# Attention followed by an expert layer on one core: weights kept as float16 pairs, one pass over the token tiles, gates 1024 wide

## The chip, the core and the metric

The program runs on one core of a Trainium2 chip. Four engines matter here. TensorE (PE) multiplies matrices into PSUM, which has eight banks of 128 x 512 float32, and its weight loads are listed apart as PEld. VectorE (DVE) and GpSimd (POOL) do arithmetic element by element, ScalarE (ACT) does functions and casts, and SyncE (SP) only issues transfers. Each engine runs its own list of instructions strictly in order, and waits on semaphores for the others.

The metric is device time in microseconds (us) of one execution. The kernel before took 1372.12 us in the median of three runs (1371.07 to 1381.09). A second listing is of one execution under the hardware profiler, whose span is 1373.2 us.

## The reference

Inputs are q, k and v of 8 batches x 8 heads x 576 positions x 64, and two expert weights in float64. What is computed, cut to the core:

```python
scores = np.matmul(q, k.transpose(0, 1, 3, 2)) / np.sqrt(64)
scores = np.where(block_i >= block_j, scores, -1e9)   # blocks of 64 positions
attn = np.exp(scores - np.max(scores, axis=-1, keepdims=True))
attn = attn / (np.sum(attn, axis=-1, keepdims=True) + 1e-09)
x = np.matmul(attn, v)            # heads side by side: 4608 tokens x 512
h = x @ w_in                      # 512 x 2048
g = h * erf(np.maximum(h, 0.0) + np.log1p(np.exp(-np.abs(h))))
out = g @ w_out                   # 2048 x 512
```

In the text, "up" is h = x @ w_in, "gate" is the step from h to g, and "down" is g @ w_out. The 2048 columns of h are 16 chunks of 128.

## The kernel before

**Precision.** Each product of the expert layer is done as three matmuls on a high and a low part: up is whi with xh, whi with xl and wlo with xh (L349), down is whi and wlo with gh, and whi with gl (L370). Parts are in fp32r, a 32-bit form of rounded float32 that TensorE reads. The high part of the gate is a cast on ACT (L336), the low part a subtraction on POOL (L337).

**Weights.** They arrive as float64, read as pairs of 32-bit integers. `load_weight` turns a block of 128 x 512 into the two parts: VectorE works on the bits in five instructions (L294, L296, L299, L302, L304), ACT squares the upper words (L298) and casts the high part (L306), POOL subtracts and adds for the low part (L307, L308). There are 32 blocks, two for each chunk.

**Gate.** The function is approximated by a tanh (L320), four squares with scale and bias on ACT (L327), one product on VectorE (L331) and a last step on VectorE that adds a constant and multiplies by h (L335). Each works on 128 x 512 elements.

**Attention.** For each head, k and q are loaded (L464 to L467), their low parts subtracted on POOL (L470, L471), and scores multiplied a first time (L482) only for the row maxima, which VectorE reduces from PSUM (L486, L512). A small transpose (L516) and a cast and a transfer on ACT's queue (L518, L519) put the negated maxima into the operand of the second product (L535, L536). ACT takes the exponential (L542) and casts to float16 (L550); the low part is subtracted on VectorE for one half of the head and on POOL for the other (L552). Probabilities times v (L582) and the row sums (L608) are done for two heads at once; ACT copies the result out (L587). For every four heads a normalisation inverts the sums, spreads them by transposes (L644), multiplies (L647), splits x (L649, L650) and stores it to memory as `x_d` (L651).

**Two passes.** Memory on chip does not hold all weights in this form. A first pass takes chunks 0 to 5 (F1 = 6) over all 18 tiles of 256 tokens, in units of two chunks (54 units, one PSUM bank each for h). It runs between the heads, tile by tile as x becomes ready, and stores a partial sum to `part_d` (L686, L687). When attention is over, its buffers are closed and the remaining weights are decoded; this stretch is called the handover. A second pass (L817 to L840) takes chunks 6 to 15 over nine tiles of 512 tokens, one chunk a unit, reads `x_d` again (L391), fetches the partial sum (L834), adds it (L839) and stores the result (L840).

**Order.** The class `Plan` writes one order for all engines: each piece of work is a task with an engine, an assumed duration, a priority and the buffers that it takes. A simulated clock goes forward, and on each free engine the ready task with the lowest priority number for which buffers are free starts next. Heads have their number as priority; units of the first pass fill what is left.

## Time and profile before

| what | before |
|---|---|
| median of three runs | 1372.12 us (1371.07 to 1381.09) |
| profiled execution, span | 1373.2 us |
| mean granted TensorE clock | 0.930 |
| moved by transfers | 179.95 MB, mean 131 GB/s |
| read from and written to main memory | 112.29 MB and 37.75 MB |
| chain that ended last, by engine | PE 39%, DVE 4%, ACT 4%, issue 1%, DMA 1% |

The busy times by engine stand in the prediction. Three rows of the span in 40 equal slices of 34.3 us each show how the load shifts. Each digit is a busy share in tenths, for PEclk the clock that TensorE was granted:

```profile
PE   7776786998998988999999979889999999999997
DVE  4899889878887887888465326983323323233232
PEclk8766687999999999899999999999999999999998
```

Heads fill slices 1 to 19 or so, the rest of the first pass slices 20 to 24, the handover is around slice 25, and the second pass has the remainder. A share of busy time is how long an engine had an instruction under way; for TensorE, whose matmuls overlap, a digit of 9 does not say that it ran at its rate.

### The profile page before, as it was taken

What the parts mean: (1) busy time and instruction counts of PE and PEld (TensorE: products, weight loads), DVE (VectorE), ACT (ScalarE), POOL (GpSimd) and SP (SyncE); (2) the same over time, 40 slices, a digit from 0 to 9 for tenths busy, and PEclk for the clock granted to TensorE, in tenths of its full rate; (3) what the DMA queues carried; (4) which work ended last, traced back from release to release, by engine and by line L of the source; (5) the groups of instructions that cost most, each with busy time, mean ns of one, the idle gap of its engine ahead of it and who ended that gap; (6) DMA issues with size and microseconds to landing.
All of it is one profiled execution on the core that took longest, in us unless ns stands there. A gap on an engine that the chain in (4) does not pass through costs nothing. (4 is left out here: it accounts for less than half of the span.)

```text
span 1373.2 us, 21951 instructions
## 1 busy us (share of the span) xinstructions
PE 1253.6 (91%) x8168; PEld 1031.3 (75%) x8168; DVE 839.3 (61%) x1268; ACT 930.3 (68%) x1685; POOL 710.2 (52%) x521
## 2 busy tenths in 40 slices
PE   7776786998998988999999979889999999999997
...
DVE  4899889878887887888465326983323323233232
...
PEclk8766687999999999899999999999999999999998
...
GB/s 234 134 153 120 197 185 121 217 196 161 207 193 159 192 202 174 171 194 152 97 150 137 187 122 115 112 45 82 123 0 123 85 39 123 62 62 123 1 62 31
DMA packets 89371, 179.95 MB, mean 131 GB/s; under 512 B 8541, under 2 KB 27293, under 8 KB 89265
## 3 DMA queue, kind: packets, MB, share of 16 engines
...
q8 instruction: 65, 1.06, 0.3%
q10 hardware_dynamic: 640, 0.17, 0.1%
...
HBM read 112.29 MB, written 37.75 MB: 109 GB/s over the span
## 5 line engine op out<-in xcount | busy, mean ns | idle before, releaser
L327 ACT ACTIVATE m_r<-m_r,c 128x512 f32<-128x512 f32 x576 | 408.8, 721 | 84.9 <-DVE m_r L331 69.7
L337 POOL TENSOR_TENSOR m_gl<-m_r,m_gh 128x512 fp32r<-128x512 f32 x144 | 193.5, 1344 | 468.8 <-ACT m_gh L336 370.6
L331 DVE SCALAR_TENSOR_TENSOR m_r<-m_r,m_r 128x512 f32<-128x512 f32 x144 | 125.8, 874 | 293.9 <-ACT m_r L327 253.9
L349 PE MATMUL m_h<-xh,whi 128*128 128x256 f32 (+1 forms) x648 | 211.7, 327 | 1.3 <-DVE mx L486 1.0
L349 PE MATMUL m_h<-xl,whi 128*128 128x256 f32 (+1 forms) x648 | 208.7, 322 | 0.0
L349 PE MATMUL m_h<-xh,wlo 128*128 128x256 f32 (+1 forms) x648 | 208.6, 322 | 0.0
L370 PE MATMUL o<-whi,m_gh 128*128 128x512 f32 x432 | 176.0, 407 | 20.7 <-ACT m_gh L336 20.7
L486 DVE TENSOR_REDUCE mx<-s 64x1 f32<-64x288 f32 (+4 forms) x384 | 162.0, 465 | 49.3 <-PE s L482 49.0
L370 PE MATMUL o<-wlo,m_gh 128*128 128x512 f32 x432 | 172.6, 400 | 0.0
L335 DVE SCALAR_TENSOR_TENSOR m_r<-m_r,m_h 128x512 f32<-128x512 f32 x144 | 98.6, 685 | 116.9 <-ACT m_r L327 116.9
L542 ACT ACTIVATE p<-t 128x288 f32<-128x288 f32 (+4 forms) x384 | 130.2, 386 | 43.6 <-PE t L536 37.0
L320 ACT ACTIVATE m_r<-m_h,c 128x512 f32<-128x512 f32 x144 | 98.7, 686 | 80.5 <-PE m_h L349 79.9
L535 PE MATMUL t<-qk 69*128 69x288 f32 (+4 forms) x384 | 132.0, 353 | 17.0 <-DMA qk<-mt 10.7
L349 PEld LDWEIGHTS m_h<-xh,whi 128*128 128x128 f32 x648 | 126.0, 194 | 13.9 <-PE t L536 1.2
L349 PEld LDWEIGHTS m_h<-xl,whi 128*128 128x128 f32 x648 | 126.0, 194 | 10.8
L349 PEld LDWEIGHTS m_h<-xh,wlo 128*128 128x128 f32 x648 | 125.4, 194 | 8.7
L370 PE MATMUL o<-whi,m_gl 128*128 128x512 f32 x432 | 128.8, 400 | 1.4 <-POOL m_gl L337 1.3
L552 POOL TENSOR_TENSOR pl<-p,ph 128x768 f16<-128x768 f32 x64 | 114.6, 1790 | 28.0 <-ACT ph L550 26.3
L482 PE MATMUL s<-qk 68*128 68x256 f32 (+3 forms) x384 | 105.3, 365 | 22.7 <-DVE mx L486 7.8
L471 POOL TENSOR_TENSOR qk<-st,qk 64x576 fp32r<-64x576 f32 x64 | 109.9, 1719 | 28.7 <-DMA qk<-qk 18.4
L536 PE MATMUL t<-qk 128*128 128x288 f32 (+4 forms) x384 | 124.4, 334 | 0.0
L470 POOL TENSOR_TENSOR qk<-st,qk 64x576 fp32r<-64x576 f32 x64 | 105.5, 1652 | 21.5 <-DMA qk<-qk 15.2
...
## 6 DMA issues: line engine op xcount, KB each, us to landing
st<-qk SPq DMA_DIRECT2D x64, 288.0 KB
qk<-qk POOLq DMA_DIRECT2D x64, 288.0 KB, 4.7
qk<-qk SPq DMA_DIRECT2D x64, 288.0 KB
...
```

What stands on the lines that cost most here:

```text
L327: add("ACT", 722, lambda r=r, a=a, pp=pp: nc.scalar.activation(r[0](), a[0](), AF.Square, bias=const(pp[1]), scale=pp[0]), r=[a[1]], w=[r[1]])
L331: add("DVE", 890, lambda r=r, a=a, c=c, pp=pp, ops=ops: nc.vector.scalar_tensor_tensor(out=r[0](), in0=a[0](), scalar=pp[0], in1=c[0](), o ...
L337: add("POOL", 1450, lambda: nc.gpsimd.tensor_tensor(out=bgl(), in0=g[0](), in1=f32(bgh()), op=ALU.subtract), r=[g[1], bgh], w=[bgl])
L349: nc.tensor.matmul(hk()[:, k, :], lhsT=a(0)[:, cc * P : (cc + 1) * P], rhs=x()[:, cc, :], start=cc == 0 and i == 0, stop=cc == NCC - 1 and ...
L370: nc.tensor.matmul(o[c](), lhsT=a()[:, sl], rhs=b_(1), start=first and k == 0 and not lo and b_ is whi, stop=last and k == nu - 1 and lo)
L470: add("POOL", 1550, lambda: nc.gpsimd.tensor_tensor(out=t[:D, 0, :], in0=st()[:D, :], in1=f32(t[:D, 2, :]), op=ALU.subtract), r=[st] + Q(n ...
L471: add("POOL", 1780, lambda: nc.gpsimd.tensor_tensor(out=t[D:, 1, :], in0=st()[D:, :], in1=f32(t[D:, 1, :]), op=ALU.subtract), r=[st], w=Q( ...
L486: add("DVE", 145 + 1.07 * w_, lambda: nc.vector.tensor_reduce(out=mx[:r, col : col + 1], in_=s()[:r, c0 : c0 + w_], axis=AX.X, op=ALU.max, ...
L535: nc.tensor.matmul(s()[:kk, :w_], lhsT=kh[:K, ks], rhs=qh[:K, q0 : q0 + w_], start=True, stop=False)
L536: nc.tensor.matmul(s()[:kk, :w_], lhsT=klh[:, ks], rhs=qhl[:, q0 : q0 + w_], start=False, stop=True)
L542: add("ACT", 160 + 0.84 * (w_ - skip), lambda: nc.scalar.activation(p32s[pt][n % NP[pt]][:kk, c : c + w_ - skip], s()[:kk, skip:w_], AF.Ex ...
L552: add(eng, ns, lambda: on.tensor_tensor(out=pl(), in0=p, in1=ph(), op=ALU.subtract), r=keys + [ph], w=[pl])
```

## The change

All 16 chunks of both weights now stay on chip in one buffer `wsb`, as scaled float16 pairs, high and low part side by side. Decoding keeps the upper 32-bit word alone: ACT scales it (L309), VectorE takes exponent bits and sign in two 16-bit instructions (L311) and joins them by a shift and an or (L313). `measure_weights` finds the largest magnitude of each of the two weights (ACT L329), from which a power of two as a scale follows; then `split_weight` writes the high part on ACT (L320) and the low part on VectorE (L321). x is stored and read as a float16 pair too, scaled by the largest v of its batch, and the scales are undone in the tanh (L374) and at the store of the result (L753).

There is a single pass: 18 tiles of 256 tokens, each in four units of four chunks (72 units). A gate is 1024 wide, with h in two PSUM banks. Its last step writes back into PSUM (L394), and ACT and VectorE take the high and low part from there (L395, L396), so POOL has no part in it. The up matmuls are at L414, the down matmuls at L429, and the result goes straight to `out` (L754). The partial sums, the second reading of x and the handover are gone.

In attention there are three buffers for k and q instead of four, and three instead of four for the float16 probabilities. The copies of the product with v move to VectorE after the first batch (L640, L642). The normalisation multiplies into PSUM (L703), casts on ACT (L705) and subtracts on VectorE (L706). The planner's assumed durations change, and it now counts VectorE as slowed while POOL works (`SHARE`).

```diff
+                        if t.shares:
+                            ns += self.SHARE * max(0.0, free_at.get("POOL", 0.0) - now)
...
-    F1 = 6
...
-    T2 = 512
...
-    NB = 4
+    NB = 3
...
+    NK = 4
+    NU = NF // NK
+    UW = NK * T
...
-    NG, NR = 4, 2
-    HT = 14
+    NG, NR = 3, 2
...
-    x_d = tc.dram_tile((2, DM, NT), F32, name="x_d")
-    part_d = tc.dram_tile((NT, DM), F32, name="part_d")
+    x_d = tc.dram_tile((2, DM, NT), F16, name="x_d")
...
+    wsb = cpool.tile([P, (2 * NF + 1) * DM], F32, name="wsb")
...
+    def home(i):
+        return wsb[:, i * DM : (i + 1) * DM]
+
+    def place(s, f):
+        return f // NK * 2 * NK + s * NK + f % NK
+
+    def wf16(s, f, lo):
+        return home(place(s, f)).bitcast(F16)[:, lo * DM : (lo + 1) * DM]
+
+    def decode(s, f):
+
...
+        add("SP", 100, lambda: nc.sync.dma_start(words(), w[f, s].bitcast(I32)), w=[raw], lag=6000.0)
+        add("ACT", 670, lambda: nc.scalar.activation(val(), f32(top()), AF.Copy, scale=2.0**-112), r=[raw], w=[k])
+        for z, (op, val16) in enumerate(((ALU.logical_shift_right, 13), (ALU.bitwise_and, 0x8000))):
+            add("DVE", 420, lambda z=z, op=op, val16=val16: nc.vector.tensor_scalar(out=sign().bitcast(U16).rearrange("p (n t) -> p n t", t=2)[:, :, z],
+                in0=words().bitcast(U16).rearrange("p (n t) -> p n t", t=4)[:, :, 1 + 2 * z], scalar1=val16, scalar2=None, op0=op), r=[raw], w=[ks])
+        add("DVE", 700, lambda: nc.vector.scalar_tensor_tensor(out=bits(), in0=bits(), scalar=3, in1=sign(), op0=ALU.logical_shift_left, op1=ALU.bitwise_or), r=[ks], w=[k])
+
+    def split_weight(s, f):
+
+        i = place(s, f)
+        sc = wrow[:, 2 * s : 2 * s + 1]
+        kw, kv = ("W", i), ("W", i + 1)
+        add("ACT", 670, lambda: nc.scalar.activation(wf16(s, f, 0), home(i + 1), AF.Copy, scale=sc), r=[kv, ("wrow", s)], w=[kw])
+        add("DVE", 700, lambda: nc.vector.scalar_tensor_tensor(out=wf16(s, f, 1), in0=home(i + 1), scalar=sc, in1=wf16(s, f, 0), op0=ALU.mult, op1=ALU.subtract),
...
+        for i, h in enumerate(hs):
+            w = UW // len(hs)
+            for b, x, y in pieces(t):
+                add("ACT", 310 + 0.84 * w * (y - x) / T, lambda i=i, h=h, b=b, x=x, y=y, w=w: nc.scalar.activation(cut(br[0]()[:, i * w : (i + 1) * w], x, y), cut(h(), x, y), AF.Tanh,
+                    bias=const(p1), scale=bsc[:, 8 * b + 4 : 8 * b + 5]), r=ks[i] + [("bt", b)], w=[(br[0], i, b)])
...
-                add("ACT", 722, lambda r=r, a=a, pp=pp: nc.scalar.activation(r[0](), a[0](), AF.Square, bias=const(pp[1]), scale=pp[0]), r=[a[1]], w=[r[1]])
+                add("ACT", 300 + 0.834 * UW, lambda r=r, a=a, pp=pp: nc.scalar.activation(r(), a(), AF.Square, bias=const(pp[1]), scale=pp[0]), r=[a] + (first if k == 0 else []), w=[r])
...
-        g = regs[-1]
-        add("DVE", 680, lambda: nc.vector.scalar_tensor_tensor(out=g[0](), in0=g[0](), scalar=fin, in1=h(), op0=ALU.add, op1=ALU.mult), r=kh, w=[g[1]])
-        add("ACT", 620, lambda: nc.scalar.copy(bgh(), g[0]()), r=[g[1]], w=[bgh])
-        add("POOL", 1450, lambda: nc.gpsimd.tensor_tensor(out=bgl(), in0=g[0](), in1=f32(bgh()), op=ALU.subtract), r=[g[1], bgh], w=[bgl])
+        r, w = regs[-1], UW // len(hs)
+        for i, h in enumerate(hs):
+            cs = slice(i * w, (i + 1) * w)
+            kh = [k for k in ks[i] if isinstance(k, tuple)]
+            add("DVE", 690, lambda cs=cs, h=h: nc.vector.scalar_tensor_tensor(out=h(), in0=r()[:, cs], scalar=end, in1=h(), op0=ALU.add, op1=ALU.mult), r=[r] + ks[i], w=kh)
+            add("ACT", 620, lambda cs=cs, h=h: nc.scalar.copy(bgh()[:, cs], h()), r=ks[i], w=[(bgh, i)])
+            add("DVE", 690, lambda cs=cs, h=h: nc.vector.tensor_tensor(out=bgl()[:, cs], in0=h(), in1=bgh()[:, cs], op=ALU.subtract), r=ks[i] + [(bgh, i)], w=[(bgl, i)])
...
+        hs = [bank(f"{name}_h{i}") for i in range(nb)]
+        hold = token("h", NH)
...
+                def go(k=k, cc=cc, f=f):
+                    for i, (lo, x) in enumerate(((0, xh), (0, xl), (1, xh))):
+                        nc.tensor.matmul(hk(k), lhsT=wf16(0, f, lo)[:, cc * P : (cc + 1) * P], rhs=x()[:, cc, :], start=cc == 0 and i == 0, stop=cc == NCC - 1 and i == 2)
+                add("PE", 3 * mmns(T, True), go, r=[("W", place(0, f)), ("Wl", place(0, f)), xh, xl], w=[(hs[k * T // 512], k), hold])
...
+                    pairs = ((gl, 0),) if lo else ((gh, 0), (gh, 1))
+
+                    def go(c=c, lo=lo, f=f, sl=sl, pairs=pairs, k=k):
+                        for a, wlo in pairs:
+                            nc.tensor.matmul(o[c](), lhsT=a()[:, sl], rhs=wf16(1, f, wlo), start=u == 0 and k == 0 and not lo and wlo == 0, stop=u == NU - 1 and k == NK - 1 and lo)
+                    add("PE", len(pairs) * mmns(DM, True), go, r=[(gl if lo else gh, k * T // 512), ("W", place(1, f)), ("Wl", place(1, f))], w=[o[c], oh[c]], off=0.001 * (8 * lo + k))
...
+            x = buf("x", [P, NCC, T], F16, nm, f"{nm}_{t}")
...
-            add("ACT", 470, lambda: nc.scalar.activation(usb()[:, q0:q1], u()[:, : q1 - q0], AF.Copy, scale=vsb()[:, :1]), r=[u, vsb], w=[(usb, hf)])
+            if qd < NQ:
+                add("ACT", 470, lambda: nc.scalar.copy(usb()[:, q0:q1], u()[:, : q1 - q0]), r=[u], w=[(usb, hf)])
+            else:
+                add("DVE", 430, lambda: nc.vector.tensor_copy(usb()[:, q0:q1], u()[:, : q1 - q0]), r=[u], w=[(usb, hf)])
...
-                add("DVE", 550 - 200 * hf, lambda q0=q0, q1=q1, rb=rb: nc.vector.tensor_tensor(out=f32(xs()[:, 1, q0:q1]), in0=usbs[pp]()[:, q0:q1], in1=rb()[:, : q1 - q0], op=ALU.mult),
-                    r=[rb, (usbs[pp], 0), (usbs[pp], 1)], w=[(xs, hf)])
-            add("DVE", 450, lambda: nc.vector.tensor_copy(xs()[:, 0, :], f32(xs()[:, 1, :])), r=[(xs, 0), (xs, 1)], w=[(xs, 2)])
...
+                add("ACT", 500 - 160 * hf, lambda q0=q0, q1=q1, rb=rb, w=w: nc.scalar.copy(x16()[:, 0, q0:q1], rb()[:, :w]), r=[rb], w=[(x16, 0, hf)])
+                add("DVE", 550 - 200 * hf, lambda q0=q0, q1=q1, rb=rb, w=w: nc.vector.tensor_tensor(out=x16()[:, 1, q0:q1], in0=rb()[:, :w], in1=x16()[:, 0, q0:q1], op=ALU.subtract),
...
+        for u in range(NU):
+            moe_unit(t, u, at[u])
...
+            add("ACT", 700, lambda ob=ob, c=c, sc=sc: nc.scalar.activation(ob(), o[c](), AF.Copy, scale=sc), r=[o[c], oh[c], *ks], w=[ob])
+            add("SP", 100, lambda ob=ob, q=q: nc.sync.dma_start(out[q : q + P, :], ob()), r=[ob], lag=3000.0)
...
+    for s in range(2):
+        for f in range(NF):
+            plan.prio = DEC0[s] + f * DECR[s]
+            decode(s, f)
+        plan.prio += 0.5 * DECR[s]
+        measure_weights(s)
+    for u in range(NU):
+        for s in range(2):
+            for f in range(u * NK, (u + 1) * NK):
+                plan.prio = MOE + u * STEP + s * DOWN - SPLIT
+                split_weight(s, f)
+
...
-            moe_unit(w2, xs[i], o, tw, 1, u, f"m2_{t}_{u}", u == 0, u == nu, u != nu, oh, 3, "g", at, 0.0)
-            if u == nu:
-                for c, pt in enumerate(pts):
-                    add("DVE", 700, lambda c=c, pt=pt, o=o: nc.vector.tensor_tensor(out=pt(), in0=o[c](), in1=pt(), op=ALU.add), r=[o[c], oh[c]], w=[pt])
-                    add("SP", 100, lambda c=c, pt=pt, t=t: nc.sync.dma_start(out[t + c * P : t + (c + 1) * P, :], pt()), r=[pt], lag=3000.0)
...
+        for t in range(NTT):
+            if t not in x1 and ready(t) <= n + 1:
+                plan.prio = n
+                x1[t] = load_x(t)
+                token_tile(t, [max(ready(t), MOE + (t * NU + u) * STEP) for u in range(NU)])
```

Three places show how the order moves. The first is VectorE early in the program. Rows name the line, the operation and output<-inputs with the shape; `mx` are row maxima, `pl` the low part of probabilities, `raw`, `bits` and `sq` a weight block on its way. Before:

```order
L552 TENSOR_TENSOR pl0_0_431<-p32_0_0_111,ph0_0_414 128x832
L512 TENSOR_TENSOR mx1_124<-mx1_124 64x1
L294 TENSOR_SCALAR bits1_0_444<-raw1_0_146 128x512
L296 SCALAR_TENSOR_TENSOR bits1_0_444<-raw1_0_146,bits1_0_444 128x512
L299 SCALAR_TENSOR_TENSOR sq1_0_353<-sq1_0_353,bits1_0_444 128x512
L486 TENSOR_REDUCE mx0_123<-s01_4_459 128x1 x2
L486 TENSOR_REDUCE mx0_123<-s2_4_464 128x1
L552 TENSOR_TENSOR pl0_1_481<-p32_0_1_112,ph0_1_454 128x832
L486 TENSOR_REDUCE mx0_123<-s3_4_466 128x1
L486 TENSOR_REDUCE mx0_123<-s4_4_0_472 64x1
```

After, from about the same head on (`sign` and `wsb` are a weight block):

```order
L311 TENSOR_SCALAR sign0_2_447<-raw0_2_143 128x512 x2
L313 SCALAR_TENSOR_TENSOR wsb_94<-wsb_94,sign0_2_447 128x512
L538 TENSOR_REDUCE mx0_123<-s01_4_422 128x1 x2
L311 TENSOR_SCALAR sign0_3_481<-raw0_3_146 128x512 x2
L313 SCALAR_TENSOR_TENSOR wsb_94<-wsb_94,sign0_3_481 128x512
L538 TENSOR_REDUCE mx0_123<-s2_4_426 128x1
L604 TENSOR_TENSOR pl0_1_498<-p32_0_1_112,ph0_1_400 128x832
L538 TENSOR_REDUCE mx0_123<-s3_4_430 128x1
L538 TENSOR_REDUCE mx0_123<-s4_4_0_440 64x1
L311 TENSOR_SCALAR sign0_4_551<-raw0_4_330 128x512 x2
L313 SCALAR_TENSOR_TENSOR wsb_94<-wsb_94,sign0_4_551 128x512
```

Before, one block is begun and its chain stands among maxima and low parts; after, three blocks pass in eleven rows, each in two rows between the maxima of heads 3 and 4, and the low part of head 1 comes behind two of them.

The second is ACT in the middle of the heads, with a gate before (`m1_5_1` is tile 5, second unit of the first pass; `t` are products to be exponentiated, `p32` their results):

```order
L320 ACTIVATE m1_5_1_r0_6670<-m1_5_1_h_6553,c1_85 128x512
L327 ACTIVATE m1_5_1_r0_6670<-m1_5_1_r0_6670,c2_87 128x512
L327 ACTIVATE m1_5_1_r1_6694<-m1_5_1_r0_6670,c3_89 128x512
L327 ACTIVATE m1_5_1_r1_6694<-m1_5_1_r1_6694,c4_91 128x512
L550 CAST ph1_45_6715<-p32_1_1_114 128x768
L542 ACTIVATE p32_1_0_113<-t1_46_128_6641 128x448
L327 ACTIVATE m1_5_1_r1_6694<-m1_5_1_r1_6694,c5_93 128x512
L320 ACTIVATE m1_5_2_r0_6740<-m1_5_2_h_6673,c1_85 128x512
L327 ACTIVATE m1_5_2_r0_6740<-m1_5_2_r0_6740,c2_87 128x512
L327 ACTIVATE m1_5_2_r1_6757<-m1_5_2_r0_6740,c3_89 128x512
L336 CAST m1_5_1_gh_6762<-m1_5_1_r1_6694 128x512
```

And after, with the gates of tile 6 (a tile that spans two batches takes two tanh instructions for each bank):

```order
L602 CAST ph0_35_7078<-p32_0_1_112 128x832
L602 CAST ph1_35_7088<-p32_1_1_114 128x768
L374 ACTIVATE m6_0_r0_7133<-m6_0_h0_7062,c1_84,bsc_98 128x2x192
L374 ACTIVATE m6_0_r0_7133<-m6_0_h0_7062,c1_84,bsc_98 128x2x64
L374 ACTIVATE m6_0_r0_7133<-m6_0_h1_7099,c1_84,bsc_98 128x2x192
L374 ACTIVATE m6_0_r0_7133<-m6_0_h1_7099,c1_84,bsc_98 128x2x64
L383 ACTIVATE m6_0_r0_7133<-m6_0_r0_7133,c2_86 128x1024
L383 ACTIVATE m6_0_r1_7185<-m6_0_r0_7133,c3_88 128x1024
L383 ACTIVATE m6_0_r1_7185<-m6_0_r1_7185,c4_90 128x1024
L374 ACTIVATE m6_1_r0_7220<-m6_1_h0_7135,c1_84,bsc_98 128x2x192
L374 ACTIVATE m6_1_r0_7220<-m6_1_h0_7135,c1_84,bsc_98 128x2x64
L383 ACTIVATE m6_0_r1_7185<-m6_0_r1_7185,c5_92 128x1024
```

The gate of 512 columns is one tanh and four squares among exponentials and casts of heads; the gate of 1024 is four shorter tanhs and squares of twice the width, and a cast of head 35 stands ahead of it.

The third is TensorE between heads. Before (`rb` are the spread sums of a normalisation, `mt` the small transpose of a head's maxima, `o1_3_0` an output bank of tile 3):

```order
L644 MATMUL rb3_1_1_0_5060<-ident_74,rw3_1_1_4982 128x128 x3
L644 MATMUL rb3_1_1_1_5064<-ident_74,rw3_1_1_4982 128x128
L644 MATMUL rb3_1_1_1_5064<-ident_74,rw3_1_1_4982 128x64
L516 MATMUL mt35_5068<-ident_74,mx1_124 5x128
L370 MATMUL o1_3_0_4948<-whi3_1350,m1_3_1_gl_4980 128x512
L582 LDWEIGHTS vh4_0_4433
L582 MATMUL u8_0_1_5078<-ph0_32_4739,vh4_0_4433 64x320
```

After, between two units of tile 4 (`t` products to be exponentiated, `s` scores for maxima, `rt` the row sums turned for a normalisation, `m4_3_h0` a bank of h):

```order
L587 MATMUL t3_29_320_5787<-qk2_105 128x256
L588 MATMUL t3_29_320_5787<-qk2_105 128x256
L534 MATMUL s01_31_5790<-qk1_104 128x256 x2
L534 MATMUL s2_31_5793<-qk1_104 128x384
L534 MATMUL s3_31_5795<-qk1_104 128x512
L534 MATMUL s4_31_0_5803<-qk1_104 64x288
L587 MATMUL t4_29_320_5805<-qk2_105 64x256
L588 MATMUL t4_29_320_5805<-qk2_105 64x256
L681 MATMUL rt3_0_5810<-sel_109,rs0_117 128x4 x3
L681 MATMUL rt3_0_5810<-sel_109,rs1_118 128x4 x3
L414 LDWEIGHTS wsb_94
L414 MATMUL m4_3_h0_5822<-xh_4_5255,wsb_94 128x256
```

Before, one down matmul stands alone between the work of heads. After, scores and products of heads 31 and 29 and a normalisation follow one another, and then the up matmuls of tile 4's last unit begin, with weights from `wsb`.

More of the change, by code (lines that the diff above doesn't have):

```diff
@@ L13 @@
 I32 = mybir.dt.int32
-U32 = mybir.dt.uint32
+U16 = mybir.dt.uint16
 F32R = mybir.dt.float32r
@@ L351, in moe_unit @@
[L351 to L352 removed]
+        for k in range(NK):
+            f = u * NK + k
             for cc in range(NCC):
[L354 to L359 removed]
```

381 lines of the change are left out of this document (153 added, 228 removed).

## The prediction

> **What bounds the kernel now.** I read the page's engine shares first, then busy time by stage, then the chain that ended last, then TensorE's timeline for what one matmul costs when nothing holds it up. The page first:
>
> ```profile
> span 1373.2 us, 21951 instructions
> PE 1253.6 (91%) x8168; PEld 1031.3 (75%) x8168; DVE 839.3 (61%) x1268; ACT 930.3 (68%) x1685; POOL 710.2 (52%) x521
> ```
>
> TensorE's 91% is not 91% of its possible rate, as matmuls overlap in the records. Busy time by stage follows (the start to head 16, the heads with the first pass between them, the handover, the second pass), and for some stages the busy time of single lines: the transposes of L516, one for each head, and the two matmul lines of the MoE.
>
> ```profile
> core 0: us, PE busy (x) PEld busy (x) DVE busy (x) ACT busy (x) POOL busy (x), PEclk, DMA share, GB/s
> 0.00:196.00 196.00, 150.78 (x1042) 109.01 (x1043) 160.05 (x246) 92.01 (x199) 139.92 (x119) 0.73 0.66 169
> 250.00:650.00 400.00, 373.74 (x3376) 314.16 (x3375) 325.61 (x552) 289.76 (x613) 300.74 (x209) 0.95 0.71 186
> 850.00:915.00 65.00, 53.19 (x213) 40.76 (x212) 61.21 (x68) 48.96 (x81) 40.48 (x28) 0.95 0.24 77
> 950.00:1350.00 400.00, 400.00 (x1767) 331.20 (x1766) 125.34 (x175) 291.14 (x443) 94.42 (x73) 1.00 0.20 69
> ```
>
> L516 in the start and with the heads, then L349 and L370 with the heads:
>
> ```profile
> 0.00:196.00 196.00, 5.74 (x17) 1.62 (x17) 0.73 0.66 169
> 250.00:650.00 400.00, 11.26 (x42) 3.53 (x42) 0.95 0.71 186
> 250.00:650.00 400.00, 79.29 (x522) 72.52 (x522) 0.95 0.71 186
> 250.00:650.00 400.00, 76.08 (x246) 43.89 (x246) 0.95 0.71 186
> ```
>
> In the second pass TensorE never rests. In the handover and at the start VectorE is the full one (61.21 of 65, 160.05 of 196). With the heads no engine is full: VectorE 81%, POOL 75%, ACT 72%. What a matmul costs in a dense stretch stands in the chain (start, length, count) and in TensorE's timeline:
>
> ```profile
> 707.48 2.89 PE m_h L349 x24
> ...
> 972.73 2.72 PE o L370 x12
> ```
>
> ```profile
> 395.73 0.33 PE L582 MATMUL u<-ph,vh 128*64 128x320 f16 x2
> 395.89 0.30 PE L582 MATMUL u<-ph,vl 128*64 128x320 f16 x2
> ...
> 396.84 0.30 PE L582 MATMUL u<-pl,vh 128*64 128x320 f16 x2
> ...
> 397.53 0.41 PE L535 MATMUL t<-qk 69*128 69x320 f32 x1
> ...
> 403.03 0.30 PE L535 MATMUL t<-qk 69*128 69x288 f32 x1
> ...
> 404.89 0.40 PE L370 MATMUL o<-whi,m_gh 128*128 128x512 f32 x1
> ...
> 409.64 1.06 PE L482 MATMUL s<-qk 68*128 68x256 f32 x6
> 410.54 0.28 PE L349 MATMUL m_h<-xh,whi 128*128 128x256 f32 x1
> ...
> 411.36 0.30 PE L582 MATMUL u<-ph,vh 128*64 128x256 f16 x2
> ...
> 411.76 0.22 PE L582 MATMUL u<-ph,vl 128*64 128x128 f16 x2
> 411.82 0.22 PE L582 MATMUL u<-pl,vh 128*64 128x128 f16 x2
> ...
> 412.91 0.33 PE L582 MATMUL u<-ph,vh 128*64 128x320 f16 x2
> ```
>
> A 512-wide fp32r matmul costs 2.72 / 12 = 226.7 ns, a 256-wide one 2.89 / 24 = 120 ns: twice the columns cost 107 ns more, so 0.417 ns a column and 13 ns fixed. The float16 pairs of 320 columns start 0.95 / 7 = 136 ns apart from 395.89 to 396.84: 133.3 ns of columns and only 2.5 fixed. One head costs TensorE 0.90 us for the six score matmuls (409.64 to 410.54), 1.86 for the probabilities and a small transpose (403.03 to 404.89), and half of 1.80 (395.73 to 397.53) and 1.55 (411.36 to 412.91) for probability times v and the sums of a pair: 4.4, with 0.2 taken for the rare transposes of the normalisation 4.6 us.
>
> So from 250 to 650 TensorE did 522 L349 matmuls at 120 ns, 246 of L370 at 227 ns and 42 heads (x522, x246, x42): 63 + 56 + 193 = 312 us of work in 400. I call that a rate share of 0.78. In the second pass it is 1767 x 226.7 ns = 400 in 400: 1.00. The loss sits where TensorE waits in order for engines that are all half busy, at the start, and in the handover.
>
> **The change, by parts.** The profiled span lies 1.1 us over the median of the runs (1372.1), so I predict against it directly. It falls into a start of 196 us, the heads with the first pass to some 650, the rest of that pass to 850, the handover to 915 and the second pass. The new span is a start, heads 17 to 63 with units between them, and the units left over.
>
> *Matmuls of the MoE.* Before there are 1296 up matmuls of 256 and 1080 of 512 columns, and 1728 down matmuls: 156 + 245 + 392 = 793 us. After there are 3456 of 256 columns and 1728 of 512, all float16: 3456 x 109.2 ns + 1728 x 215.8 ns = 377 + 373 = 750 us. Gain 43 us where TensorE is full. The 256-wide tiles load twice the weights per column of the second pass; in the rows at 411.76 and 411.82 two loads and two 128-column matmuls take 0.06 us, so a load hides under 109 ns.
>
> *The start.* VectorE sets it. The price of the old decoding, by block and by shape:
>
> ```profile
> L296 DVE SCALAR_TENSOR_TENSOR bits<-raw,bits 128x512 int32<-128x512 int32 x32 | 42.5, 1328 | 0.9
> L299 DVE SCALAR_TENSOR_TENSOR sq<-sq,bits 128x512 f32<-128x512 f32 x32 | 40.0, 1250 | 2.1 <-ACT sq L298 0.8
> ...
> L294 DVE TENSOR_SCALAR bits<-raw 128x512 int32<-128x512 int32 x32 | 34.5, 1078 | 1.1 <-DMA raw<-w 1.1
> ...
> L304 DVE SCALAR_TENSOR_TENSOR bits<-raw,bits 128x512 f32<-128x512 uint32 x32 | 31.7, 990 | 0.9
> ...
> L302 DVE TENSOR_SCALAR bits<-sq 128x512 int32<-128x512 int32 x32 | 20.6, 645 | 0.9
> ```
>
> That is 5.29 us a block, and 8 of the 32 blocks lie in the first 196 us. The new chain is two halves of 512 in 16 bits (nearest L302, 0.645), one shift-and-or and later one subtraction (nearest L304, 0.99, without POOL less: I take 0.85). By the order after, all 32 decodings, some 12 subtractions, 17 heads and two gates stand on VectorE before head 17, where the units flow on TensorE. Before, 160 us in 196 held 8 blocks (42) and 17 heads, so 6.9 us a head; after: 17 x 6.9 + 32 x 2.14 + 12 x 0.85 + 8 = 204 us, and at the 82% that VectorE reached before (160.05 of 196) 249. POOL no longer splits weights there, so I take 245 instead of 196: 49 us lost. Ends: 204 if VectorE were full, 283 if each of the three operations of a block cost as L296 (32 x 0.85 more, at 82%).
>
> *Heads 17 to 63.* By the order after, TensorE now has 2496 up and 1224 down matmuls there: 273 + 264 + 46 x 4.6 = 748 us. Is another engine longer? The rows:
>
> ```profile
> L327 ACT ACTIVATE m_r<-m_r,c 128x512 f32<-128x512 f32 x576 | 408.8, 721 | 84.9 <-DVE m_r L331 69.7 <-ACT m_r L327 0.4
> ...
> L331 DVE SCALAR_TENSOR_TENSOR m_r<-m_r,m_r 128x512 f32<-128x512 f32 x144 | 125.8, 874 | 293.9 <-ACT m_r L327 253.9 <-POOL m_gl L337 39.9
> ...
> L320 ACT ACTIVATE m_r<-m_h,c 128x512 f32<-128x512 f32 x144 | 98.7, 686 | 80.5 <-PE m_h L349 79.9
> L335 DVE SCALAR_TENSOR_TENSOR m_r<-m_r,m_h 128x512 f32<-128x512 f32 x144 | 98.6, 685 | 116.9 <-ACT m_r L327 116.9
> ...
> L336 ACT CAST m_gh<-m_r 128x512 fp32r<-128x512 f32 x144 | 87.8, 610 | 23.0 <-DVE m_r L335 19.7 <-PE o L370 3.2
> ...
> L542 ACT ACTIVATE p<-t 128x448 f32<-128x448 f32 x64 | 34.4, 537 | 9.5 <-PE t L536 8.6
> ...
> L542 ACT ACTIVATE p<-t 128x192 f32<-128x192 f32 x64 | 21.0, 327 | 2.1 <-PE t L536 1.8
> ```
>
> An ACT element costs (537 - 327) / 256 = 0.82 ns, so a 1024-wide square 721 + 420 = 1.14 us, and the gate of a unit 2 x 0.686 + 4 x 1.14 + 2 x 0.61 = 7.2 us, where two old gates took 8.4. ACT's own work for a head is at most the page's 930 less the gates' 595, over 64: 5.2. Each head also queues a small DMA on ACT, and the next operation waits for it:
>
> ```profile
> 342.11 0.70 ACTq L519 DMA_DIRECT2D qk<-mt  x1
> 342.85 0.26 ACT L518 CAST mt<-mt 5x128 fp32r<-5x128 f32 x1 [0.77 <-ACT mt L518]
> ```
>
> So at most 51 x 7.2 + 46 x 5.9 + 18 for the stores = 657 us: 88% of TensorE's 748. VectorE takes the subtraction for the low half over from POOL (L337 goes): 51 x (1.2 + 4 x 0.685) + 46 x 6.9 = 518. The normalisation, once for a pair of heads, drops a cast and POOL's subtraction and adds two subtractions on VectorE and two casts on ACT; the two copies of u move from ACT to VectorE after the first batch. Four more VectorE operations a pair, each at most L335's 0.685, are 63 us over 46 heads: 581, 78%. ACT's two casts take the place of the two copies. POOL, 75% before, loses its work for the MoE. TensorE is the fullest, and its units stand ready from earlier tiles. The query and key buffers go from four to three, so a head's loads start two heads ahead instead of three:
>
> ```profile
> qk<-qk POOLq DMA_DIRECT2D x64, 288.0 KB, 4.7
> ```
>
> 4.7 us to land, a copy after it and POOL's subtractions fit into two heads of 17 us, so I cost it at nothing; if heads came every 6 us it would show. The share lies between 0.78 (before, with heads) and 1.00 (second pass). I take 0.94, nearer the second, since TensorE now queues and the others wait: 748 / 0.94 = 796 us.
>
> *The rest.* After the last head's transpose stand 816 up and 456 down matmuls: 89 + 98 + some 7 of attention = 194, at 0.99 196. A gate (from its second half 0.7 + 3.5 + 1.2 + 1.1 + 0.7 + 0.6, about 8 us) hides under the 10.4 us of one up and one down between a unit's own two; if ACT is late, TensorE waits there. No handover, no second pass, no partial sums through memory; DMA falls to one reading of x in float16, and is no bound (0.71 of its share with the heads before). The load of x for tile 15 waits on SP behind the last stores of x; ahead of it TensorE has three blocks of 5.2 us, against some 12 of normalisation and two transfers, so 0 to 10 us, taken as 0. The last gate uncovers some 4 us, and a store follows: 10.
>
> Sum: 245 + 796 + 196 + 10 = 1247 us.
>
> One rule weighs against this. The Trainium skill, "TensorE: Matmul & The Clock Gate", section "Back-to-back issue gap", says that a stream of weight load and matmul pairs holds some 81 ns a matmul at 128 columns where the streaming alone is 56, so that loads show. Taken as 25 ns on each of 5184 matmuls it would make the sum 1247 + 130 = 1377; the rows at 411.76 and 411.82 (0.06 us with two loads) disagree.
>
> **Rivals.** *Slower: the share stays at 0.78.* Two 1024-wide units hold four of eight PSUM banks, the outputs two or three more; a head's matmuls find one or two, so TensorE stands in order behind an exp or a max. For it: 0.78 with smaller units. Against: there VectorE and POOL were 81% and 75% full, and lose that. Price 748 / 0.78 = 959, time 1410 (959 + 451); it decides against the change below a share of 0.81 (1373) and is slower by over 1% below 0.80.
>
> *In between: share 0.81 to 0.87*, by ACT's long gate squares standing in order ahead of an exp that TensorE waits for: ACT is second at up to 88%. Against: it has a tenth to spare. 1310 to 1373.
>
> *Faster: share 0.98 and VectorE full at the start*: 204 + 763 + 194 + 6 = 1167. For it: the second pass's 1.00. Against: VectorE was never full at the start.
>
> *Weight loads show.* If float16 with a load per matmul keeps the 13 ns of fp32r, 5184 x 10.5 ns = 54 us more: 1301. For it: no row shows a 128-column float16 load under 256 columns; against, the pairs above.
>
> *The change does nothing of the sort*: ruled out, the order after has one up and one down per tile and chunk.
>
> **How the numbers follow.** Forecast (share 0.88 to 0.97, start 225 to 270): 0.57, own range 1200 to 1325. Fast rival 0.11. In between 0.14, of which 0.03 within 1%. Loads show 0.06. Share under 0.81: 0.12, of which 0.09 slower by over 1%. The range 1165 to 1350 leaves out about 0.04 below and 0.16 above. A difference of 1% is about what a measurement of this kernel can tell. Faster 0.85, same 0.06, slower 0.09.
>
> **What would show it.** Right: float16 pairs at 109 and 216 ns in the last 190 us; head 17's transpose at 225 to 270 us with VectorE over 75% before it; a head every 17 us after; no part_d or second reading of x. Wrong: spacings over 115 ns; waits of TensorE on ACT (exp) or VectorE (max) of over 100 us in the middle; ACT over 95% there; TensorE's clock under 0.95 after 250 us.

## The result, and the profile after

The changed kernel took 1312.91 us in the median of four runs (1309.82 to 1316.28), against 1371.59 us for the kernel before (1369.07 to 1381.09 in four): a ratio of 0.9553, 95% interval 0.9517 to 0.9589. It is 59 us faster where 125 us were forecast. 1312.9 us lies in the range given (1165 to 1350), but the gain is less than half of the one forecast. The profiled execution has a span of 1308.0 us.

The changed kernel's page, its engine shares, the granted clock in 40 slices of 32.7 us, and what the transfers moved:

```profile
PE 1192.5 (91%) x9254; PEld 835.8 (64%) x9254; DVE 778.4 (60%) x1433; ACT 895.5 (68%) x1485; POOL 348.8 (27%) x280
PEclk8667676889999999999999999999999999999999
DMA packets 69468, 123.38 MB, mean 94 GB/s; under 512 B 7073, under 2 KB 34017, under 8 KB 69360
HBM read 74.52 MB, written 18.87 MB: 71 GB/s over the span
```

TensorE is again at 91%, ACT as before at 68%, POOL at 27% for 52%. Transfers moved 123 MB for 180. The clock row shows the kernel's weak place: all of its low digits lie in the first nine slices.

Busy time by stage of the changed kernel (start to head 17's small transpose, head 17 to 18, heads 18 to 63, the rest):

```profile
core 0: us, PE busy (x) PEld busy (x) DVE busy (x) ACT busy (x) POOL busy (x), PEclk, DMA share, GB/s
0.00:260.60 260.60, 181.89 (x1207) 125.08 (x1207) 196.05 (x375) 145.97 (x293) 99.17 (x96) 0.72 0.62 166
260.60:314.00 53.40, 42.44 (x308) 26.78 (x306) 29.29 (x42) 37.32 (x49) 9.60 (x6) 0.87 0.19 44
314.00:1100.00 786.00, 767.74 (x6330) 550.20 (x6330) 476.34 (x910) 565.61 (x957) 236.74 (x177) 0.99 0.35 92
1100.00:1308.00 208.00, 200.45 (x1418) 133.76 (x1414) 76.69 (x108) 146.63 (x188) 3.28 (x2) 0.99 0.07 24
```

Against the sum of the prediction: the start is 260.6 us for 245, heads 17 to 63 are 839 for 796 (260.6 to 1099.6), and the rest is 208 for 196 + 10. So nearly all of the miss lies in the first two.

To see where TensorE's time goes, every matmul of a trace was given its price (those of the prediction: 0.4167 ns a column, with 13 ns for fp32r and 2.5 for float16, float16 matmuls that run beside each other in parts of the array counted once, and 109 ns, an estimate, for the small fp32 ones that the prediction did not price singly). What a stage has over the sum of its matmuls is called lost: gaps, waits, and matmuls at a lower clock alike. Each row is one execution, and those of the changed kernel lie up to 6.5 us apart, so that a few us say little; and the planner writes a new order for each kernel, so that a run differs in more than its edit. For the two kernels and all runs below with units, in us ("h17" is head 17's small transpose; "expert" and "attention" are TensorE's work from head 17 to head 63, and in warm17 the fillers count as work):

```
run           h17 at  lost before  17 to 63  expert  attention  lost   span
before         196.0        100.3     454.5   129.2      218.1  107.2  1373.2
after          260.6        142.7     839.0   536.7      219.3   83.1  1308.0
nb3c           248.2        142.4     855.3   547.1      221.0   87.2  1312.0
nb4            304.7        167.2     805.8   516.3      220.0   69.5  1317.4
no_decode      225.9        108.8     833.2   536.7      220.0   76.3  1267.4
light_gate     258.2        138.0     799.2   536.7      217.0   45.4  1261.2
down195        262.0        145.7     817.7   532.8      218.2   66.7  1290.7
tuned          255.0        150.8     802.1   528.8      220.0   53.2  1271.3
no_low         242.5        150.1     834.4   547.1      181.4  106.0  1282.4
light_nolow    251.2        144.9     769.8   536.7      177.9   55.1  1223.2
nk2            259.4        147.3     810.3   540.2      215.8   54.3  1279.5
warm17         242.5        117.3     853.5   547.1      221.0   85.2  1302.8
nk2_tuned      270.2        143.1     731.5   479.4      219.0   33.2  1240.6
```

The first two rows, with what comes after head 63 up to the last matmul's end, are the balance of the change: matmul work fell from 1111 to 1071 us, all of it expert matmuls (791 to 750), and the loss from 257 to 232 us. Behind head 63 the loss fell from 49 to 7 us and with the heads by 24, but the start gave 42 back.

### The profile page after: what moved, and what is told of

Its sections match the earlier page's. It is cut to its first block, busy times and chain, and to the rows that moved or that the text cites. A ratio compares the mean times of both kernels' runs of the same rounds, so it can differ in the third digit from the quotient of the medians.

```text
span 1308.0 us, 23297 instructions
## 1 busy us (share of the span) xinstructions
PE 1192.5 (91%) x9254; PEld 835.8 (64%) x9254; DVE 778.4 (60%) x1433; ACT 895.5 (68%) x1485; POOL 348.8 (27%) x280
## 4 chain that ended last, share of the span: by engine, by line
PE 75%; DVE 5%; ACT 3%; issue 1%; DMA 1%; POOL 1%; ACTq 0%; POOLq 0%; DVEq 0%
PE o L429 28%; PE m_h L414 27%; PE u L634 5%; PE t L587 3%; PE t L588 3%; PE s L534 3%; PE us L663 2%; ACT m_r L383 1%; PE rt L681 1%; DMA qk<-qk 1%; PE rb L699 1%; DVE mx L538 1%; DVE m_r L387 1%; ACT p L594 1%; POOL pl L604 1%
## 5 line engine op out<-in xcount | busy, mean ns | idle before, releaser
L414 PE MATMUL m_h<-xh,wsb 128*128 128x256 f16 x2304 | 399.5, 274 | 2.1 <-DVE mx L538 1.6
L414 PEld LDWEIGHTS <-wsb 128*128 128x128 f16 x3456 | 333.1, 98 | 55.7 <-issue 5.5
L429 PE MATMUL o<-wsb,m_gh 128*128 128x512 f16 x1152 | 344.0, 390 | 20.1 <-ACT m_gh L395 14.7
L383 ACT ACTIVATE m_r<-m_r,c 128x1024 f32<-128x1024 f32 x288 | 330.7, 1148 | 37.5 <-DVE m_r L387 29.2
L414 PE MATMUL m_h<-xl,wsb 128*128 128x256 f16 x1152 | 315.4, 274 | 0.0
L429 PE MATMUL o<-wsb,m_gl 128*128 128x512 f16 x576 | 211.2, 387 | 0.0
L429 PEld LDWEIGHTS <-m_gh 128*128 128x128 f16 x1152 | 107.9, 100 | 140.7 <-ACT m_gh L395 20.8
L387 DVE SCALAR_TENSOR_TENSOR m_r<-m_r,m_r 128x1024 f32<-128x1024 f32 x72 | 95.1, 1320 | 152.4 <-ACT m_r L383 152.3
L374 ACT ACTIVATE m_r<-m_h,c,bsc 128x512 f32<-128x512 f32 (+3 forms) x192 | 123.1, 669 | 40.4 <-PE m_h L414 40.2
L394 DVE SCALAR_TENSOR_TENSOR m_h<-m_r,m_h 128x512 f32<-128x512 f32 x144 | 92.8, 690 | 39.1 <-ACT m_r L383 38.7
L602 ACT CAST ph<-p 128x832 f16<-128x832 f32 (+1 forms) x128 | 109.1, 856 | 3.1 <-ACT mt L570 1.5
L395 ACT CAST m_gh<-m_h 128x512 f16<-128x512 f32 x144 | 82.1, 587 | 36.5 <-DVE m_h L394 35.6
```

Source lines behind the costliest of these rows:

```text
L374: add("ACT", 310 + 0.84 * w * (y - x) / T, lambda i=i, h=h, b=b, x=x, y=y, w=w: nc.scalar.activation(cut(br[0]()[:, i * w : (i + 1) * w], ...
L383: add("ACT", 300 + 0.834 * UW, lambda r=r, a=a, pp=pp: nc.scalar.activation(r(), a(), AF.Square, bias=const(pp[1]), scale=pp[0]), r=[a] + ...
L387: add("DVE", 160 + 1.05 * UW, lambda r=r, a=a, c=c, pp=pp, ops=ops: nc.vector.scalar_tensor_tensor(out=r(), in0=a(), scalar=pp[0], in1=c() ...
L414: nc.tensor.matmul(hk(k), lhsT=wf16(0, f, lo)[:, cc * P : (cc + 1) * P], rhs=x()[:, cc, :], start=cc == 0 and i == 0, stop=cc == NCC - 1 a ...
L429: nc.tensor.matmul(o[c](), lhsT=a()[:, sl], rhs=wf16(1, f, wlo), start=u == 0 and k == 0 and not lo and wlo == 0, stop=u == NU - 1 and k = ...
L602: add("ACT", 850, lambda: nc.scalar.copy(ph(), p), r=keys, w=[ph])
```

## The experiments

Expectations that give VectorE 84% and 220 us before head 17, or ACT 82 to 87% with heads, add instructions up by their lengths; the view by stage counts overlapping ones once, and has 196 us (75%) and 72%.

**Buffers for q and k.** Four buffers do not fit beside the weights, so a control gave room first, and the second run differs from it in one number.

```diff
-    NG, NR = 3, 2
+    NG, NR = 2, 2
...
-NPH = 3
+NPH = 2
...
-        st = buf("a", [P, S], F32, "st", f"st_{n}", 2)
+        st = buf("a", [P, S], F32, "st", f"st_{n}", 3)
```

> Control for the run with four buffers: the changed kernel with three buffers for q and k, but two instead of three buffers for the gate's float16 pair, two instead of three for the float16 probabilities and three instead of two for the loaded q and k, so that the two differ in one number. Both theories: within 25 us of the changed kernel's 1308, the fewer buffers costing 0 to 25 us in the stage with heads.

```diff
-    NB = 3
+    NB = 4
```

> The control with four buffers for q and k instead of three. Theory (VectorE sets the start; 84% busy up to head 17 in the changed kernel): head 17's small transpose within 10 us of the control's and the span within 12 us. Rival (the three buffers hold back the heads of the start; GpSimd's load waited 66 us between 40 and 250 us for the previous reader): head 17 earlier by 20 to 60 us and the span shorter by 20 to 45 us.

The control's span was 1312.0 us, that with four buffers 1317.4, as the theory had it; but head 17 came at 304.7 us for 248.2, which neither forecast had. With four, more units stand ahead of head 17 (46.5 us of expert matmuls for 15.7), so the loss before it is the better measure: 167 us for 142. With the heads it was 69.5 us for 87.2. The three buffers are not what holds the start, and for the span costing them at nothing was right.

**VectorE's part of the decoding left out** (sign, exponent bits and their joining).

```diff
-        for z, (op, val16) in enumerate(((ALU.logical_shift_right, 13), (ALU.bitwise_and, 0x8000))):
...
-        add("DVE", 700, lambda: nc.vector.scalar_tensor_tensor(out=bits(), in0=bits(), scalar=3, in1=sign(), op0=ALU.logical_shift_left, op1=ALU.bitwise_or), r=[ks], w=[k])
```

> Leaves out VectorE's three instructions for each weight block in the decoding (sign and exponent bits, and their joining), so the weights are not the reference's; loads and ACT's part stay. That is 39.5 + 32.3 = 72 us of VectorE's 220 before head 17. Theory (VectorE sets the start): head 17's small transpose moves from 260.6 us to 175 to 215, the span to 1230 to 1268. Rival (buffers or transfers set the start): head 17 after 240 us, span over 1285.

Its two stages, to head 17 and from there to head 63:

```profile
0.00:225.90 225.90, 172.06 (x1202) 120.44 (x1202) 140.34 (x284) 149.48 (x294) 96.51 (x96) 0.78 0.71 194
225.90:1059.10 833.20, 811.66 (x6636) 578.62 (x6634) 504.15 (x946) 598.89 (x1004) 244.32 (x183) 0.98 0.34 90
```

The span fell by 41 us, to 1267.4, and head 17 came at 225.9 us, between the two forecasts. VectorE's busy time up to head 17 fell by 56 us (196.05 to 140.34) and its share to 62%, so it is a cause of the long start but not its only bound.

**Heads alone, and heads with the loads of the weights.** The first leaves out the expert layer; the second adds the 32 loads and nothing else.

```diff
-    for s in range(2):
-        for f in range(NF):
-            plan.prio = DEC0[s] + f * DECR[s]
-            decode(s, f)
...
-                token_tile(t, [max(ready(t), MOE + (t * NU + u) * STEP) for u in range(NU)])
```

> Leaves out all of the expert layer (weights, units and their gates); attention with its normalisation and the store and reading of x stay, and x's high part is copied to the output. VectorE has then 6.9 us a head. Theory (decoding on VectorE slows the heads of the start): head 17's small transpose at 130 to 180 us. Rival (a head's own chain of load, maxima, exponentials sets the pace of the start): head 17 after 210 us, and heads go on at 13 us or more each.

```diff
+            add("SP", 100, lambda raw=raw, s=s, f=f: nc.sync.dma_start(raw().bitcast(I32), w[f, s].bitcast(I32)), w=[raw], lag=6000.0)
+            add("ACT", 230, lambda raw=raw, s=s, f=f: nc.scalar.copy(wmx[:, 12 * s : 12 * s + 1], raw()[:, 1:2]), r=[raw], w=[("wmx", s)])
```

> Attention alone as before, and with it the 32 loads of the weights at their places in the order, each read by a copy of one column on ACT (nothing is decoded, no unit runs, and x's high part is copied to the output). Heads alone had head 17's small transpose at 180 us; with all but VectorE's part of the decoding it was at 226 us, in the changed kernel at 260.6. Theory (instructions of the decoding and the first units on VectorE and ACT slow the start, not the transfers): head 17 within 12 us of 180. Rival (16.8 MB of loads delay the transfers of q and k): head 17 at 205 us or later.

Heads alone to head 17 and to head 63, columns as above:

```profile
0.00:180.20 180.20, 143.13 (x1076) 104.99 (x1077) 111.54 (x233) 84.19 (x192) 100.85 (x98) 0.76 0.64 157
180.20:641.60 461.40, 344.61 (x2790) 274.84 (x2788) 296.89 (x659) 233.17 (x537) 244.00 (x180) 0.72 0.62 159
```

And heads with the loads, to head 17:

```profile
0.00:200.30 200.30, 148.46 (x1082) 109.25 (x1084) 108.50 (x237) 92.19 (x228) 99.13 (x98) 0.73 0.80 224
```

Alone, heads come every 10.0 us (461.4 / 46), with VectorE at 64%, ACT at 51% and no engine near full. That looks like the pace of a head's own chain under this order; what in the chain sets it was not tested. Head 17 comes at 180.2 us then, at the edge of the theory and far from the rival. The loads bring it to 200.3, between the two forecasts: they cost some 20 us in the start, in one run of each. Whether they delay the transfers of q and k, or hold ACT, is open: its copies stand in order behind the loads, and it waited 31 us for them in these 200. So the start is a ladder: 180 heads, 200 with the loads, 226 with ACT's decoding, the low parts and the first units too, 261 with VectorE's decoding. The runs do not separate ACT from the units in the third step.

**Fillers against the low clock of the start.**

```diff
-        if n < 8:
+        if n < 17:
             lists.append(([warm] * WARM, 0, 1, 1.0))
```

> Ten filler matmuls also in heads 8 to 16 (90 more, some 19 us of TensorE at full clock). Theory (the granted clock of 0.6 to 0.8 in the start comes from gaps on TensorE, and matmuls at half clock lengthen each head's chain): the clock of the first 250 us rises over 0.85 and the span falls by 10 to 30 us to 1278 to 1298. Rival (the start is order and VectorE; the fillers only take TensorE's idle time): within 8 us of 1308, or longer.

The clock of the first 250 us rose from 0.71 to 0.74 only, and the span was 1302.8 us: the rival's.

**A light gate**, without three of its four squares and its product.

```diff
-PROG = [('S', 0), ('S', 1), ('S', 2), ('M', 3, 1), ('S', 4)]
+PROG = [('S', 0)]
...
+    pars = pars[-1:]
```

> Leaves out three of the four squares and the product of the gate (the function is then not the reference's): 250 us less on ACT and 95 us less on VectorE, nothing less on TensorE. Theory (from 314 us on TensorE is full with its own work, a head costing it 5.6 us there): only the waits for the gate go, and the span falls by 13 to 38 us to 1270 to 1295. Rival (TensorE loses its time with heads to waits for ACT and VectorE): at least half of the 83 us lost between 260 and 1100 us goes and the span is below 1260.

```profile
258.20:1057.40 799.20, 792.88 (x6560) 573.02 (x6560) 436.03 (x892) 432.92 (x849) 232.38 (x181) 0.99 0.36 93
```

The span was 1261.2 us, past the theory's end and not quite at the rival's. With the heads 83.1 us of loss became 45.4: TensorE stood without a record for 6 us of 799, where it was 29 of 839 in the changed kernel (53.4 + 786.0, less 42.44 and 767.74, in its view by stage). So 38 us of the loss went with the larger part of the gate. TensorE's list of waits names less (us in total, times, longest): its rows for the gate's results in the changed kernel, from 260 to 314 us and from 314 to 1100 us, and with the light gate from 260 to 1050 us.

```profile
PE o L429 <- ACT m_gh L395: 8.4, 2, 4.5
...
PE o L429 <- DVE m_gl L396: 3.1, 1, 3.1
...
PE o L430 <- ACT m_gh L396: 0.9, 1, 0.9
...
PE o L430 <- DVE m_gl L397: 0.3, 1, 0.3
```

That is some 12 us for 1, and most of it stands between heads 17 and 18. Where the loss lies says more. From head 20 on, with the same prices, it is 62 to 65 us in all five runs with this gate and these priorities (after, nb3c, nb4, no_decode, warm17), and 39 us here: 23 us less. Between heads 17 and 20 the same five lose 5 to 24 us, so the other 15 of the 38 us are not clear of what a shifted order does there. ACT's load and the gate's length both shrank here; the next runs part them.

**The order alone: down matmuls later behind their up matmuls.**

```diff
-GATE, DOWN = 0.2, 1.5
+GATE, DOWN = 0.2, 1.95
```

> One number: DOWN, by which the down matmuls of a unit stand behind its up matmuls in the planner's priorities, is 1.95 instead of 1.5. No engine gets less work. Theory after the light gate (38 of the 83 us that TensorE loses with heads are waits for the gate, whose results the order wants too early): the loss with heads falls by 20 to 40 us and the time to 1268 to 1292. Rival (the gain of the light gate came from ACT and VectorE having less work, not from its length): within 12 us of the changed kernel's 1308 to 1313.

1292.03 us (1286.89 to 1295.22), ratio to before 0.9441 (0.9367 to 0.9515). With no engine relieved the loss with heads fell by 16 us, to 66.7 (from head 20 on to 49 us): less than forecast, but it comes from the order and not from a load. The wait at its worst, in the changed kernel (TensorE in order of time: start, length, count, and in brackets what it stood idle for):

```profile
266.95 1.07 PE L534 MATMUL s<-qk 68*64 68x288 f32 x4
272.47 1.89 PE L429 MATMUL o<-wsb,m_gh 128*128 128x512 f16 x4 [4.45 <-ACT m_gh L395]
274.15 0.63 PE L429 MATMUL o<-wsb,m_gl 128*128 128x512 f16 x1
274.58 1.06 PE L429 MATMUL o<-wsb,m_gh 128*128 128x512 f16 x2
275.43 0.63 PE L429 MATMUL o<-wsb,m_gl 128*128 128x512 f16 x1
275.86 1.03 PE L429 MATMUL o<-wsb,m_gh 128*128 128x512 f16 x2
276.71 0.39 PE L429 MATMUL o<-wsb,m_gl 128*128 128x512 f16 x1
...
277.59 0.59 PE L429 MATMUL o<-wsb,m_gh 128*128 128x512 f16 x2
278.02 0.38 PE L429 MATMUL o<-wsb,m_gl 128*128 128x512 f16 x1
278.24 0.59 PE L429 MATMUL o<-wsb,m_gh 128*128 128x512 f16 x2
```

ACT in the same stretch of the changed kernel:

```profile
268.24 0.83 ACT L602 CAST ph<-p 128x768 f16<-128x768 f32 x1 [0.77 <-ACT mt L570]
269.40 1.15 ACT L383 ACTIVATE m_r<-m_r,c 128x1024 f32<-128x1024 f32 x1 [0.34 <-DVE m_r L387]
271.22 0.72 ACT L320 ACTIVATE wsb<-wsb,wrow 128x512 f16<-128x512 f32 x1 [0.67 <-DVE wsb L321]
271.85 1.16 ACT L395 CAST m_gh<-m_h 128x512 f16<-128x512 f32 x2
```

The last square, then a weight block's cast, then the gate's own cast, and TensorE stands in order for 4.45 us before the down matmuls that need it. It then pays again: the ten matmuls of 512 columns from 272.47 to 276.71 take 0.42 us each, at 278.02 it is 0.22, so some 2 us more. The Trainium skill, "TensorE: Matmul & The Clock Gate", section "What's actually happening", has the array fall to half its clock after an idle window of some 3.4 us and return after a busy one; this stretch agrees, with 4.45 us idle and about as long at half rate.

**More of the order.** DOWN as above, with the first decoding earlier, fewer fillers and small shifts.

```diff
-GATE, DOWN = 0.2, 1.5
-DEC0, DECR, SPLIT = (0.5, 6.5), (0.35, 0.4), 0.8
-MOE, STEP = 12.0, 0.93
+GATE, DOWN = 0.347, 1.950
+DEC0, DECR, SPLIT = (-0.57, 6.50), (0.347, 0.400), 0.80
+MOE, STEP = 12.00, 0.944
...
-    WARM = 10
+    WARM = 4
```

> DOWN as in the run before, and the first weights' decoding one head earlier (DEC0 -0.57), 4 instead of 10 filler matmuls in each of the first heads, and small shifts of four more of the planner's numbers (GATE 0.347, STEP 0.944, PV -0.93, the row maxima's transpose 0.03 later). The work of each engine is the same but for 48 filler matmuls. Theory (part of the 142 us that TensorE loses before head 17 is order too): 10 to 25 us less than with DOWN alone, 1245 to 1280. Rival (the start is set by the work of VectorE and the length of a head's chain alone): within 8 us of DOWN alone.

1268.10 us (1263.61 to 1273.11), ratio 0.9273 (0.9209 to 0.9337): the size that the theory gave, but not its reason. The loss before head 17 did not fall (150.8 us for 145.7); the gain is 10 us of fillers and 13 us of loss with heads, less those 5.

**Less attention work for TensorE**, once with the gate as it is and once with the light gate: the second score matmul is left out.

```diff
-                nc.tensor.matmul(s()[:kk, :w_], lhsT=klh[:, ks], rhs=qhl[:, q0 : q0 + w_], start=False, stop=True)
```

> Leaves out the second score matmul with the low parts of q and k (precision is lost), 0.85 us of TensorE's work for each head, 39 us for heads 17 to 63; the subtractions that feed it stay. Theory (TensorE is full from head 18 on, and a head costs it 5.6 us): the time from head 18 to head 63 falls by 30 to 40 us. Rival (TensorE loses that time to waits anyway): it falls by less than 15 us.

> The light gate without the second score matmul (both left out, and one of the planner's numbers, DRAIN, at -0.75 instead of -0.70). The earlier run without that matmul took 38 us of work from TensorE and gave 31 of it back as waits. Theory (there ACT, at 84 to 87%, was the next bound; with the light gate it is at 65% and TensorE is the only one near full): against the light gate, the sum of TensorE's expert work and the time from head 18 to 63 falls: with the units equal, 25 to 40 us less. Rival (the chain of a head, not ACT, gives the pace): less than 15 us less.

Between head 18 and head 63 the changed kernel has 785.8 us, 505.4 of them expert matmuls; without the second matmul it is 809.9 with 536.7. Beside the units that leaves 280.4 and 273.2 us: 38 us of work were taken away and 7 us gained. With the light gate the same step goes from 259.7 (791.2 less 531.5) to 223.3 us (728.7 less 505.4): 36 us gained. So over the stretch that both expectations name the rival held in the first run, the theory in the second. The stretch matters, as from head 17 to head 18 the four kernels take 53, 25, 8 and 41 us: counted from head 17, as in the table, the step gains 15 us (302.3 to 287.3) and 29 us (262.5 to 233.1). With the heavy gate more than half of what was taken from TensorE came back as loss (83.1 us to 106.0), with the light one a quarter (45.4 to 55.1). That fits a TensorE that waits for the gate.

**Gates 512 wide again**, the rest of the change kept.

```diff
-    NK = 4
+    NK = 2
...
-MOE, STEP = 12.0, 0.93
+MOE, STEP = 12.0, 0.465
...
-    NG, NR = 3, 2
+    NG, NR = 6, 2
...
-    NH = 2
+    NH = 4
```

> Undoes one part of the change: gates 512 wide again (two chunks a unit, 144 units), with twice as many buffers of half the size for h and the float16 pair, two of half the size for the gate's intermediate values, and half the planner's step from unit to unit; the weights stay on chip and the pass is one. Two squares of 512 take 2 x 0.721 us where one of 1024 takes 1.148, so ACT has some 85 us more and VectorE some 31 us more. Theory (TensorE waits with heads for the length of the gate, which is 4.2 us of ACT instead of 7.2): the loss with heads falls by 15 to 40 us and the time to 1268 to 1298. Rival (ACT, at 82 to 86% with heads, is what TensorE waits for): 1320 to 1365.

```profile
259.40:1069.70 810.30, 800.65 (x6544) 576.38 (x6544) 506.37 (x1001) 649.60 (x1219) 233.98 (x181) 0.99 0.35 91
```

1278.59 us (1276.41 to 1281.26), ratio 0.9295 (0.9269 to 0.9320). ACT is fuller, 80% (649.6 of 810.3) for 72%, and the kernel is 34 us faster; the loss with heads is 54 us for 83 (41 from head 20 on), and TensorE's list of waits has no row for the gate's results. So ACT's load is not what TensorE waits for. What fits this run, the light gate and the later down matmuls alike is the time that a gate takes against the time that the order gives it between a unit's up and down matmuls; a unit here is also half as large, which no run parts from the gate's length. The 1024-wide gate, one of the three parts of the change, costs 34 us in this order.

**Both together**, the diff against the kernel with 512-wide gates.

```diff
-GATE, DOWN = 0.2, 1.5
-DEC0, DECR, SPLIT = (0.5, 6.5), (0.35, 0.4), 0.8
-MOE, STEP = 12.0, 0.465
+GATE, DOWN = -0.018, 1.757
+DEC0, DECR, SPLIT = (-0.83, 4.72), (0.474, 0.142), 2.69
+MOE, STEP = 10.73, 0.500
...
-    WARM = 10
-    NH = 4
-    NO = 3
...
+    WARM = 2
+    NH = 3
+    NO = 2
```

> Gates 512 wide as in the run that undid the 1024, and the planner's numbers shifted: DOWN 1.757, GATE -0.018, units from head 10.73 on instead of 12, the weights of the second matrix decoded from head 4.72 at 0.142 instead of 6.5 at 0.4, two filler matmuls instead of ten, and four small ones. No engine's work changes but for 64 filler matmuls. Theory (what TensorE loses in the start and to the gate is order for the most part): 15 to 45 us less than with 512-wide gates alone, 1233 to 1264. Rival (what is left is work): within 10 us of 1278.6.

Its stage with heads, and its page:

```profile
270.20:1001.70 731.50, 731.50 (x6184) 524.87 (x6183) 480.18 (x952) 592.44 (x1129) 239.25 (x183) 1.00 0.39 101
```

```profile
PE 1150.6 (93%) x9190; PEld 818.6 (66%) x9190; DVE 784.3 (63%) x1505; ACT 948.0 (76%) x1773; POOL 342.2 (28%) x280
```

1242.47 us (1242.11 to 1243.00), ratio to before 0.9074 (0.9044 to 0.9105), the fastest here that computes the whole function. TensorE has a record at every moment with heads, and the loss there is 33 us. The loss before head 17 is as large as ever (143 us), but 50 us of expert matmuls lie in that stretch for 26, and so come off the end.

## Why the prediction missed

*The matmuls* were right. A 512-wide float16 matmul starts every 0.22 us (278.02 to 278.24), and 256-wide ones keep 109 ns:

```profile
1150.00 0.27 PE L414 MATMUL m_h<-xl,wsb 128*128 128x256 f16 x1
1150.11 0.38 PE L414 MATMUL m_h<-xh,wsb 128*128 128x256 f16 x2
1150.33 0.27 PE L414 MATMUL m_h<-xl,wsb 128*128 128x256 f16 x1
```

Three in 0.33 us, each with its own load of 128 columns: loads stay hidden, and the rival by which they show is out. So is the rule from the Trainium skill, "TensorE: Matmul & The Clock Gate", section "Back-to-back issue gap", in the way the prediction priced it.

*The start* was mis-sized by 16 us. VectorE's work was right, 196 us for the 204 forecast; what failed is "at the 82% that VectorE reached before": it reached 75%. VectorE was not the whole bound that the prediction made it: without its decoding head 17 still comes at 226 us, where heads alone have a pace of 10 us each and the loads add some 20 us.

*Heads 17 to 63* is the step that failed most: "The share lies between 0.78 (before, with heads) and 1.00 (second pass). I take 0.94, nearer the second, since TensorE now queues and the others wait." The work was right, 756 us for 748. The share was 0.90 (756 / 839): 83 us lost for 48. What failed is the reason "TensorE now queues and the others wait": the others had even less work than priced (from 260.6 to 1099.6 us VectorE 506 us for 581, ACT 603 for 657), and TensorE waited for them all the same. The light gate has 754 / 799 = 0.94, so the number was one for a gate that is hardly waited for. The prediction hid the gate under a unit's matmuls in the last stage and gave it no price with heads, where casts, exponentials and weight blocks stand between its squares. With the light gate 38 us of the loss go, 23 of them clear of the start, and 45 stay.

*The rest* was right, 208 us for 206.

*The rivals.* "In between" named the long squares and 1310 to 1373 us; the median is at its edge. It had the right instructions and the wrong reason, ACT at 88% and an exponential behind the squares: 512-wide gates fill ACT more and are faster, and with heads TensorE's list of waits has 4 us for exponentials and 12 for the gate. So the sign named as wrong, over 100 us of waits on exponentials or maxima, could not show this miss. That the share stays at 0.78 was wrong; VectorE fell from 81% to 61% there and POOL from 75% to 30%, as argued, but no run tests that this is why. The fast rival's 0.98 no run reached; the best, the one with both, has 0.955.

*What stays open:* which part of the third step of the start's ladder is ACT's and which the units', why heads 17 to 20 lose so unequally, and what the 45 us are that stay with the light gate; small gaps at the many changes between kinds of matmuls are likely, and no run shows it.
